# MLP2's finish: x added by accumulating transfers for the first two token blocks and half of the third, where VectorE added half, half and all

## The chip, the core and the metric

The kernel runs on one core of a Trainium2 chip. The metric is the device time of one execution in microseconds (us). TensorE (PE) multiplies, VectorE (DVE) and ScalarE (ACT) do the elementwise work, SyncE (SP) only issues transfers, and GpSimd (POOL) does nothing here but issue transfers of another kind: those that add what they bring to what lies in the destination.

## The reference

All tensors are float32; x has 2048 tokens of width 512.

```
xn = layernorm(x)
a  = xn @ dft_hid_re.T ; b = xn @ dft_hid_im.T
s  = dft_seq_re @ a - dft_seq_im @ b
h  = relu(xn @ w1 + b1) ** 2          # 512 -> 1792
g  = silu(h @ w2 + b2)                # 1792 -> 512
out = x + s * g
```

## The kernel before

Every operand is held as a high and a low part (`split`: ACT writes the high part, L69, DVE the low one, L72), and a product is three matmuls: high by high, high by low, low by high (`PASSES`). On top of that the large products are made blockwise, with seven products of sums of quarter blocks where eight would stand (`PRODUCTS`); the sums of operands (L201 to L209) and of results (`combine`, L240 to L243) are DVE's.

The order is written out by hand; each engine goes through its own list in order. First come the Fourier part (`products`, `mm`, `stage2`), which leaves s in four DRAM tiles `Y`, then MLP1 (`hidden`), which leaves the squared relu in DRAM tiles `HD`, and last MLP2, the loop over `units` from L785 on. It runs over four token blocks c of 512 tokens, and in each over seven slices p of 256 hidden features; n counts the 28 units. A unit is 42 matmuls (`outer`, L595) that need the unit's operand. `operand` makes it: SP loads it (`hr`, L566), DVE makes sums (L207 to L209), and ACT and DVE split it (L69, L72) into one of three places of the tile `block`. So at most three operands stand ready, and the seven results of a token block are summed up in PSUM over its seven units.

At the end of a token block, `combine` turns the seven sums into four quarters, k = 0 to 3, in the tile `z` (called `e` in the code, tag "e"): first ACT copies one sum into it (L239), then DVE does L240 to L243. The tile has a single buffer. The copy for the next block waits until all four quarters of the previous one are in DRAM. Behind this copy ACT writes the bias into the banks of the next block (L588); PE's second product of the block waits for one of those, for `m_b2` (shown as m_b_o) in blocks 1 and 2, and for the bank pair `m_12` (shown as m) in block 3.

A block's quarters are finished during the next block (`finish`): silu on ACT (L636), times s on DVE (L640), and then x is added in one of two ways. If x was loaded by `load_fin`, DVE adds it and SP issues the transfer to `out` (`plus`, L645 and L646). If not, POOL issues a transfer that adds x from DRAM into the quarter (L628), and SP issues the transfer to `out` later, at a place of its own (`put`, L631), once the adding transfer has landed. Before, k = 0 and 1 of blocks 0 and 1 and all of block 2 went the first way, and k = 2 and 3 of blocks 0 and 1 the second. The finish of block 2 thus lies in block 3, between the operands that PE needs there. Block 3 has a written-out tail (`rest`, `step`) with all four quarters on DVE.

Of the kernel before, what the change touches and what calls it, by code (L numbers as in the profile page):

```python
# [19 lines left out]
NTC = S // TC  # L20
# [42 lines left out]
def fnet_gated_kernel(ctx, tc, x, xt, ct, wd, w1, w2, b1, b2, out):  # L63
# [23 lines left out]
    def bank(tag, name):  # L87

        n = {"b3": 3, "b2": 2}.get(tag, 1)
        return acc.tile([P, n, 512], F32, tag=tag, name=name)  # L90

    def buf(tag, shape, name, dtype=F32, bufs=1):
        return pool.tile(shape, dtype, tag=tag, bufs=bufs, name=name)
# [383 lines left out]
    def load_w1(p):  # L477
        if p < NP - 1:
            t = sixth(2 + p, 2)
            nc.sync.dma_start(t.bitcast(F32), W1D[p])  # L480
            W1[p] = [t[:, :, n] for n in range(7)]
        else:
            a = buf("g0b", [P, 2, 3, 256], f"w1a_{p}", F32R)
            b = buf("g1b", [P, 2, 4, 256], f"w1b_{p}", F32R)
            nc.sync.dma_start(a.bitcast(F32), W1D[p][:, :, 0:3])
            nc.sync.dma_start(b.bitcast(F32), W1D[p][:, :, 3:7])
            W1[p] = [a[:, :, n] for n in range(3)] + [b[:, :, n] for n in range(4)]
# [96 lines left out]
    def bias(m, n, cols=slice(0, 2)):  # L584

        m = m.rearrange("p (k e) -> p k e", k=2)[:, cols]
        b = BIASED[n] * 256
        nc.scalar.activation(m, b2s[:, None, b:b + 256].to_broadcast([P, cols.stop - cols.start, 256]), AF.Copy)  # L588
# [13 lines left out]
    def at(src, k):  # L602

        h, b = WHERE[k]
        return src.rearrange("(h k p) (b e) -> h b p k e", h=2, k=2, b=2)[h, b]

    def load_fin(c):

        fin[c] = []
        for n, src in enumerate((Y[c], x[c * TC:(c + 1) * TC])):  # L610
            for m in range(2 if n == 0 or c > NTC - 3 else 1):
                tag = f"pq{n}{m}" if c < NTC - 1 else (("g0a", "sx"), ("g0b", "pq10"))[n][m]
                t = buf(tag, [P, 2, 512], f"fin{c}_{n}{m}")
                for i in range(2):
                    nc.sync.dma_start(t[:, i].rearrange("p (k e) -> p k e", k=2), at(src, 2 * m + i))
                fin[c].append(t)
# [13 lines left out]
    def put(c, e, k):  # L630
        nc.sync.dma_start(at(out[c * TC:(c + 1) * TC], k), e[:, k].rearrange("p (k e) -> p k e", e=256))  # L631
# [76 lines left out]
    def go(*names):  # L708


        for v in names:
            k, n = v[0], int(v[1:])
            if k == "m":
                load_rows(n, buf("pq00", [P, 4, 256], f"rows{n}"))
            elif k == "l":
                load_w2(n)
            elif k != "h" or n < len(units):
                if v not in making:
                    making[v] = {"h": lambda: operand(n, *units[n]), "x": lambda: tokens(n // 2, n % 2),
                                 "w": lambda: late_w2(n)}[k]()  # L720
                next(making[v])
# [28 lines left out]
    c = NTC - 1  # L750
# [8 lines left out]
    with ordered:  # L759
        before = None  # L760
        for n, (c, p) in enumerate(units):
            ahead, behind = beside.get((c, p), ((), ()))
            go(*ahead)
            unit = hidden(n, c, p)
            next(unit)
            if before:
                next(before)
            next(unit)
            go(*behind)
            before = unit  # L770
            if n == 0:
                stage2(NC - 1, 0)
                stage2(NC - 1, 1, "ba")
            if c == 0 and p + 4 < NP:
                load_w1(p + 4)
            if n == len(units) - 1:

                m26, m4 = bank("b2", "m_b2_o0"), bank("ba", "m_ba_o0")
                bias(m26[:, 0], 2)
                bias(m4[:, 0], 4)  # L780
        m753, m1 = bank("b3", "m_b3_o0"), bank("bb", "m_bb_o0")
        bias(m753[:, 1], 5)
        next(before)

        for n, (c, p) in enumerate(units):  # L785
            last = c == NTC - 1
            if n == 0:
                ms = m26, m753, m4[:, 0], m1[:, 0]
                at_ = product
            elif not last and p == 0:  # L790

                m4, m26, m753, m1 = (bank(tag, f"m_{tag}_o{c}") for tag in (("bb", "ba")[c - 1], "b2", "b3", "bc"))
                ms = m26, m753, m4[:, 0], m1[:, 0]
                bias(ms[2], 4)
                bias(product(ms, 2), 2)
                bias(product(ms, 5), 5)
            elif p == 0:

                m5, m40 = (bank(tag, f"m_{tag}_last")[:, 0] for tag in ("bb", "bc"))
                m12, m67 = bank("b2", "m_12"), bank("b3", "m_67")  # L800
                m3 = bank("ba", "m_ba_last")[:, 0]
                m4 = m40, m67[:, 2]
                ms = {1: m12[:, 0], 2: m12[:, 1], 6: m67[:, 0], 7: m67[:, 1], 5: m5, 3: m3}
                at_ = dict.__getitem__
                bias(m5, 5)
                bias(m40, 4, slice(0, 1))
                bias(ms[2], 2)
                bias(m4[1], 4, slice(1, 2))

            def add(k, p):  # L810
                if last and k == 4:
                    for i in range(2):
                        outer(m4[i], k, ready[c, p], p, (i,))
                else:
                    outer(at_(ms, k), k, ready[c, p], p)

            go(*{0: ("l4",), 1: ("w6",), 2: ("l5",)}.get(n, ()))
            if not last or p < REST:
                for k in ORDER if p else FIRST_LAST if last else FIRST:
                    add(k, p)  # L820
            if n == 1:

                nc.scalar.activation(stats[:, 0, 0, 0:1], stats[:, 0, 0, 0:1], AF.Silu)
            go(f"h{n + 3}")
            if p == NP - 1 and not last:
                e = buf("e", [P, 4, 512], f"z{c}")
                combine(e, ms)
                done_next = c, e
            if c and not last and p in (3, 4):
                put(*done, p - 1)  # L830
            go(f"h{n + 2}", *{2: ("w6",), 3: ("w6",)}.get(n, ()), f"h{n + 6}")
            if p == (3 if last else 5):
                load_fin(c)
            if p == NP - 1 and not last:
                done = done_next
            elif c:
                for k in ((2, 3), (0,), (1,), (), (), (), ())[p] if not last else ((), (0,), (1, 2), (3,), (), (), ())[p]:
                    finish(*done, k)


        e = buf("g1a", [P, 4, 512], f"z{c}")
        tail = NP - 1
        whole = slice(0, 512)
        w = [slice(i * 256, (i + 1) * 256) for i in range(2)]

        def rest(ks, ps=range(REST, NP)):
            for k in ks:
                for f in ps:
                    add(k, f)

        def step(to, a, b, op, w=whole):
            nc.vector.tensor_tensor(e[:, to, w], a[:, w], e[:, b, w], op=op)

        rest((1, 2, 6), range(REST, tail))
        rest((1, 2), (tail,))
        nc.scalar.activation(e[:, C21], ms[1], AF.Copy)
        step(C11, ms[2], C21, ALU.add)
        silu(e, C11)
        times(c, e, C11)
        plus(c, e, C11)  # L860
        rest((6,), (tail,))
        rest((7,))
        step(C22, ms[6], C21, ALU.add)
        step(C21, ms[7], C22, ALU.subtract)
        rest((5,))
        step(C12, m5, C22, ALU.subtract)
        step(C22, m5, C21, ALU.add)
        silu(e, C22)
        rest((3,))
        for f in range(REST, NP):  # L870
            outer(m4[0], 4, ready[c, f], f, (0,))
        times(c, e, C22)
        plus(c, e, C22)
        step(C12, m3, C12, ALU.add)
        silu(e, C12)
        step(C21, m4[0], C21, ALU.subtract, w[0])
        silu(e, C21, one)
        for f in range(REST, NP):
            outer(m4[1], 4, ready[c, f], f, (1,))
        times(c, e, C12)  # L880
        step(C21, m4[1], C21, ALU.subtract, w[1])
        silu(e, C21, two)
        times(c, e, C21, one)
        plus(c, e, C21, one)
        times(c, e, C21, two)
        plus(c, e, C21, two)
        plus(c, e, C12)
# [43 lines left out]
```

## Time and profile before

| | us |
|---|---|
| median of 3 runs (710.11, 710.51, 713.1) | 710.51 |
| the profiled execution's own time | 710.93 |
| its span, first to last instruction | 709.1 |
| PE busy, of the span | 687.0 |
| DVE busy | 584.5 |
| ACT busy | 347.3 |
| POOL, first accumulating transfer / last | 606.27 / 644.24 |
| MLP2's blocks 1, 2, 3 begin on PE at | 595.71, 630.57, 664.03 |

PE and DVE are so full that a difference can only come from a place where one waits for the other. A timeline row gives start, duration, engine, line, operation and tiles; in brackets stands how long the engine had been idle before it, and who ended that. In a windows row, after the stretch and its length, stand the busy time of PE, weight loads, DVE, ACT and POOL, then the TensorE clock that was granted (1.00 is full speed), and the DMA engines' share and rate.

### The profile page before, as it was taken

What the parts mean: (1) busy time and instruction counts of PE and PEld (TensorE: products, weight loads), DVE (VectorE), ACT (ScalarE), POOL (GpSimd) and SP (SyncE); (2) the same over time, 40 slices, a digit from 0 to 9 for tenths busy, and PEclk for the clock granted to TensorE, in tenths of its full rate; (3) what the DMA queues carried; (4) which work ended last, traced back from release to release, by engine and by line L of the source; (5) the groups of instructions that cost most, each with busy time, mean ns of one, the idle gap of its engine ahead of it and who ended that gap; (6) DMA issues with size and microseconds to landing.
All of it is one profiled execution on the core that took longest, in us unless ns stands there. A gap on an engine that the chain in (4) does not pass through costs nothing.

```text
span 709.1 us, 12790 instructions
## 1 busy us (share of the span) xinstructions
PE 687.0 (97%) x5179; PEld 647.7 (91%) x5179; DVE 584.5 (82%) x886; ACT 347.3 (49%) x475; POOL 5.2 (1%) x8
## 2 busy tenths in 40 slices
PE   8999999999999999999999998999999999999985
PEld 5778788999999999999999988899999998999985
DVE  7999654779598798797897737889999879999995
ACT  4437332444453544543543325667777754454431
POOL 0000000000000000000000000000000000101000
PEclk9999999999999999999999999999999999999998
DMA  9522441533653653835746809966724995667642
GB/s 333 216 90 90 155 131 42 216 108 138 214 204 134 254 177 134 310 112 194 262 122 233 328 11 366 351 223 208 269 119 164 350 417 193 187 218 208 239 149 88
DMA packets 55018, 141.09 MB, mean 199 GB/s; under 512 B 5040, under 2 KB 21680, under 8 KB 53680
## 3 DMA queue, kind: packets, MB, share of 16 engines
q1 hardware_dynamic: 49840, 124.56, 49.6%
q10 hardware_dynamic: 4032, 14.68, 5.1%
q0 software_dynamic: 1088, 1.05, 1.0%
q8 instruction: 40, 0.66, 0.4%
q14 instruction: 18, 0.15, 0.1%
HBM read 97.00 MB, written 43.27 MB: 198 GB/s over the span
## 4 chain that ended last, share of the span: by engine, by line
PE 73%; DVE 16%; DMA 6%; issue 2%; ACT 2%; SPq 0%; DVEq 0%; ACTq 0%
PE m_b L300 23%; PE yps L287 12%; PE hps L541 7%; PE m_b_o L595 7%; PE m_bb L300 5%; PE m_ba L300 5%; PE hps_b L541 4%; DVE block L72 4%; PE pq_b L353 3%; DMA w1b<-w1d 3%; PE hps_ba L541 2%; DVE g L72 2%; DMA w2raw<-in_w 2%; PE m_bc_o L595 1%; DMA xr<-in_xt 1%
## 5 line engine op out<-in xcount | busy, mean ns | idle before, releaser
L300 PE MATMUL m_b<-g,block 128*128 128x256 f32 x1080 | 129.0, 276 | 0.0
L300 PEld LDWEIGHTS m_b<-g,block 128*128 128x128 f32 x1080 | 125.5, 188 | 0.0
L69 ACT ACTIVATE g<-r 128x768 fp32r<-128x768 f32 (+2 forms) x65 | 57.4, 885 | 82.9 <-PE m_b L300 38.7
L72 DVE TENSOR_TENSOR g<-r,g 128x768 fp32r<-128x768 f32 (+2 forms) x65 | 65.5, 1007 | 36.0 <-ACT g L69 35.8
L287 PE MATMUL yps<-wd,pq 128*128 128x512 f32 (+1 forms) x414 | 92.9, 374 | 0.0
L287 PEld LDWEIGHTS yps<-wd,pq 128*128 128x128 f32 x414 | 74.8, 188 | 14.0
L72 DVE TENSOR_TENSOR g<-t,g 128x1024 fp32r<-128x1024 f32 x48 | 58.7, 1222 | 12.1 <-ACT g L69 12.1
L541 PE MATMUL hps<-xT,block 128*128 128x256 f32 x504 | 59.9, 278 | 0.0
L541 PEld LDWEIGHTS hps<-xT,block 128*128 128x128 f32 x504 | 58.7, 188 | 0.2
L69 ACT ACTIVATE g<-t 128x1024 fp32r<-128x1024 f32 x48 | 50.3, 1048 | 14.3 <-PE m_ba L300 6.5
L353 PE MATMUL pq_b<-g,block 128*128 128x512 f32 x180 | 47.6, 398 | 1.8 <-DVE g L72 1.7
L595 PE MATMUL m_b_o<-w,block 128*128 128x256 f32 x360 | 44.0, 278 | 2.3 <-ACT m_b_o L588 2.3
L552 ACT ACTIVATE h<-h,b1s 128x512 f32<-128x512 f32 x56 | 37.3, 715 | 18.1 <-DVE h L242 17.8
L300 PE MATMUL m_b<-g,xc 128*128 128x256 f32 x360 | 45.1, 277 | 0.0
L595 PEld LDWEIGHTS m_b_o<-w,block 128*128 128x128 f32 x360 | 42.2, 188 | 2.9 <-ACT m_b_o L588 2.9
L69 ACT ACTIVATE block<-hr 128x768 fp32r<-128x768 f32 (+1 forms) x28 | 35.5, 1268 | 18.4 <-DVE hr L209 9.3
L353 PEld LDWEIGHTS pq_b<-g,block 128*128 128x128 f32 x180 | 32.9, 188 | 11.3 <-DVE g L72 2.4
L300 PEld LDWEIGHTS m_b<-g,xc 128*128 128x128 f32 x360 | 42.9, 188 | 0.3
L72 DVE TENSOR_TENSOR block<-hr,block 128x768 fp32r<-128x768 f32 (+1 forms) x28 | 41.6, 1485 | 0.9 <-ACT block L69 0.8
L201 DVE TENSOR_TENSOR t<-r 128x512 f32<-128x512 f32 x48 | 32.9, 685 | 4.1 <-DMA r<-in_ct 3.9
L541 PE MATMUL hps_b<-xT,block 128*128 128x256 f32 x288 | 35.1, 278 | 0.0
L541 PEld LDWEIGHTS hps_b<-xT,block 128*128 128x128 f32 x288 | 34.1, 188 | 0.0
(200 smaller groups left out, 1182.6 us busy)
## 6 DMA issues: line engine op xcount, KB each, us to landing
r<-in_ct SPq DMA_DIRECT2D x63, 512.0 KB, 3.5
hd<-h ACTq DMA_DIRECT2D x28, 512.0 KB, 4.9
hr<-hd SPq DMA_DIRECT2D x28, 512.0 KB, 4.5
w1d<-w0g SPq DMA_DIRECT2D x21, 512.0 KB, 3.1
block<-w1d SPq DMA_DIRECT2D x6, 1792.0 KB, 8.8
block<-w2d SPq DMA_DIRECT2D x3, 1792.0 KB, 14.7
y<-ysb SPq DMA_DIRECT2D x16, 256.0 KB, 3.0
fin<-y SPq DMA_DIRECT2D x16, 256.0 KB, 4.5
```

What stands on the lines that cost most here:

```text
L69: nc.scalar.activation(hi, src, AF.Copy)
L72: return nc.vector.tensor_tensor(lo, src, hi.bitcast(F32), op=ALU.subtract)
L201: nc.vector.tensor_tensor(t[:, 0:2], r[:, 0:1].to_broadcast([P, 2, 256]), r[:, 1:3], op=ALU.add)
L287: nc.tensor.matmul(ps[:, s], PQ[c, m, k // 2][:, a_, w:w + P], WD[m, k][:, b_, s], start=n == 0, stop=n > len(todo) - 3, skip_group_check= ...
L300: nc.tensor.matmul(ps[:, d * CW:(d + 1) * CW], w[:, a_, d * P:(d + 1) * P], mv(b_), start=first and d == 0 and (a_, b_) == (HI, HI), stop= ...
L353: nc.tensor.matmul(accs[c][k], w, g[:, b_, 2 * h:2 * h + 2], start=j == 0 and h == 0 and (a_, b_) == (HI, HI), stop=j == NJ - 1 and h == 1 ...
L541: nc.tensor.matmul(product(ms, k), W1[p][a][:, a_, q * P:(q + 1) * P], xT[c, q][:, b_, b], start=share not in first, stop=q == 1 and (a_, ...
L552: nc.scalar.activation(x_[:, s], x_[:, s], AF.Relu, bias=b1s[:, f:f + 1])
L595: nc.tensor.matmul(m[:, k * 256:(k + 1) * 256], g[:, a_, a, k * P:(k + 1) * P], W2[p][:, b_, b], start=p == 0 and k == 0 and (a_, b_) == ( ...
```

## The change

Blocks 0 and 1 load no x for VectorE any more, and block 2 half of it; the finish of the third block begins with the two quarters that go by transfer; and the places of `put` are new.

```
-            for m in range(2 if n == 0 or c > NTC - 3 else 1):
+            for m in range(2 if n == 0 else (0, 0, 1, 2)[c]):
...
-            if c and not last and p in (3, 4):
-                put(*done, p - 1)
+            if c:
+                for k in ({4: (2,), 5: (3,)} if last else {3: (2, 3), 4: (0,), 5: (1,)}).get(p, ()):
+                    put(*done, k)
...
-                for k in ((2, 3), (0,), (1,), (), (), (), ())[p] if not last else ((), (0,), (1, 2), (3,), (), (), ())[p]:
+                for k in ((2, 3), (0, 1), (), (), (), (), ())[p] if not last else ((), (2,), (3, 0), (1,), (), (), ())[p]:
```

On POOL, whose list is nothing but these transfers (z0, z1, z2 are the tiles of blocks 0, 1, 2), the difference is this.

```order
-L628 DMA z0_6394<-in_x 128x2x256 x2
-L628 DMA z1_6785<-in_x 128x2x256 x2
-L902 UNCONDITIONAL_BRANCH
...
+L628 DMA z0_6391<-in_x 128x2x256 x4
+L628 DMA z1_6779<-in_x 128x2x256 x4
+L628 DMA z2_7171<-in_x 128x2x256 x2
+L903 UNCONDITIONAL_BRANCH
```

Four transfers of 256 KB became ten.

On SP, from the last operand load of block 1 (`hr1_6`) to the loads for the next finish, before (the number after hr is the block, the next one the slice):

```order
L566 DMA hr1_6_6460<-hd1_6_940 128x1024
L566 DMA hr2_0_6516<-hd2_0_941 128x1024
L646 DMA out_0<-z0_6394 128x2x256
L566 DMA hr2_1_6572<-hd2_1_942 128x1024
L646 DMA out_0<-z0_6394 128x2x256
L631 DMA out_0<-z0_6394 128x2x256
L566 DMA hr2_2_6628<-hd2_2_943 128x1024
L631 DMA out_0<-z0_6394 128x2x256
L566 DMA hr2_3_6678<-hd2_3_944 128x1024
L566 DMA hr2_4_6728<-hd2_4_945 128x1024
L615 DMA fin1_00_6730<-y1_67 128x2x256 x2
```

And with the change:

```order
L566 DMA hr1_6_6457<-hd1_6_940 128x1024
L566 DMA hr2_0_6513<-hd2_0_941 128x1024
L566 DMA hr2_1_6571<-hd2_1_942 128x1024
L631 DMA out_0<-z0_6391 128x2x256 x2
L566 DMA hr2_2_6624<-hd2_2_943 128x1024
L631 DMA out_0<-z0_6391 128x2x256
L566 DMA hr2_3_6674<-hd2_3_944 128x1024
L631 DMA out_0<-z0_6391 128x2x256
L566 DMA hr2_4_6725<-hd2_4_945 128x1024
L615 DMA fin1_00_6727<-y1_67 128x2x256 x2
```

The last transfer of z0 to `out` moved from ahead of `hr2_3` to behind it, and all four are now `put`s that wait for an accumulating transfer. The order for z1 in block 2 changes in the same way.

On DVE, in block 3, between the low parts of the operands of slices 4 (`hr3_4`) and 5 (`hr3_5`), before (fin2_00 and fin2_01 hold s, fin2_10 and fin2_11 hold x):

```order
L72 TENSOR_TENSOR block_78<-hr3_4_7120,block_78 128x1792
L640 TENSOR_TENSOR z2_7180<-z2_7180,fin2_00_7122 128x512
L645 TENSOR_TENSOR z2_7180<-z2_7180,fin2_10_7128 128x512
L640 TENSOR_TENSOR z2_7180<-z2_7180,fin2_01_7125 128x512
L645 TENSOR_TENSOR z2_7180<-z2_7180,fin2_11_7131 128x512
L207 TENSOR_TENSOR hs3_6_7401<-hr3_6_7249 128x512
...
L72 TENSOR_TENSOR block_78<-hr3_5_7188,block_78 128x1792
```

And with the change:

```order
L72 TENSOR_TENSOR block_78<-hr3_4_7114,block_78 128x1792
L640 TENSOR_TENSOR z2_7171<-z2_7171,fin2_01_7119 128x512
L640 TENSOR_TENSOR z2_7171<-z2_7171,fin2_00_7116 128x512
L645 TENSOR_TENSOR z2_7171<-z2_7171,fin2_10_7122 128x512
L207 TENSOR_TENSOR hs3_6_7390<-hr3_6_7240 128x512
...
L72 TENSOR_TENSOR block_78<-hr3_5_7179,block_78 128x1792
```

One addition (L645) is gone here, and one more ahead of `hr3_4`; the multiplications (L640) all stay.

## Prediction

> **What bounds the kernel now.** I read the busy shares first, then the windows by stage, then the timeline where PE has a hole. PE is the bound of the whole:
>
> ```profile
> PE 687.0 (97%) x5179; PEld 647.7 (91%) x5179; DVE 584.5 (82%) x886; ACT 347.3 (49%) x475; POOL 5.2 (1%) x8
> ```
>
> The change touches only MLP2 from its second token block on. These two windows are blocks 1 and 2, and block 3 with the tail:
>
> ```profile
> 594.60:663.40 68.80, 67.85 (x594) 67.38 (x594) 65.99 (x86) 33.29 (x38) 4.99 (x4) 1.00 0.68 200
> 663.40:709.10 45.70, 36.30 (x301) 35.71 (x300) 36.09 (x50) 14.66 (x20) 0.00 (x0) 0.92 0.47 160
> ```
>
> In blocks 1 and 2 PE lacks 0.95 us of 68.8, and that lies where block 1 begins, ahead of any line changed. DVE work taken out of these blocks buys nothing. Block 3's window lacks 9.4 us, most of it behind PE's last matmul, and its clock is 0.92. PE's timeline shows a hole within:
>
> ```profile
> 684.03 0.39 PE L595 MATMUL m<-w,block 128*128 128x256 f32 x2
> 686.76 0.74 PE L595 MATMUL m<-w,block 128*128 128x256 f32 x4 [2.34 <-DVE block L72]
> 687.33 0.84 PE L595 MATMUL m<-block 128*128 128x256 f32 x6
> 688.01 1.28 PE L595 MATMUL m<-w,block 128*128 128x256 f32 x6
> 689.09 1.48 PE L595 MATMUL m<-block 128*128 128x256 f32 x6
> 690.37 3.51 PE L595 MATMUL m<-w,block 128*128 128x256 f32 x24
> 693.72 0.84 PE L595 MATMUL m<-block 128*128 128x256 f32 x6
> ```
>
> PE arrives at 684.42 and waits 2.34 us for the low part of slice 5's operand. After that it is slow. The fine windows say why:
>
> ```profile
> 595.00:600.00 5.00, 4.05 (x33) 3.65 (x32) 4.76 (x6) 1.41 (x3) 0.00 (x0) 1.00 0.88 290
> ...
> 686.70:688.00 1.30, 1.24 (x10) 1.24 (x11) 1.26 (x4) 0.00 (x0) 0.00 (x0) 1.00 1.00 316
> 688.00:690.00 2.00, 2.00 (x13) 2.00 (x12) 2.00 (x3) 0.00 (x0) 0.00 (x0) 0.56 0.88 269
> 690.00:692.00 2.00, 2.00 (x12) 2.00 (x12) 0.04 (x1) 0.00 (x0) 0.00 (x0) 0.59 1.04 347
> 692.00:694.00 2.00, 2.00 (x20) 2.00 (x19) 0.07 (x1) 0.60 (x1) 0.00 (x0) 1.00 0.42 148
> ```
>
> The granted clock falls to about half from 688.0 for some 3.4 us, just behind the hole. The hole of 0.95 us in the first row cost no clock. The chain of waits gives the normal pace, and what carries the end after the hole:
>
> ```profile
> 655.35 3.40 PE m_b_o L595 x30
> ...
> 693.30 0.61 ACT z L856
> ```
>
> At 3.40/30 = 0.113 us each, the 46 matmuls from 686.76 to 693.72 need 5.21 us; they took 6.96. The slow clock cost 1.75 us. From 693.30 the chain runs through ACT and DVE, which start when PE's first products are done, so all that PE wins by then reaches the end.
>
> **What the change removes.** These DVE rows are the path to that hole:
>
> ```profile
> 663.55 1.22 DVE L241 TENSOR_TENSOR z<-m_b_o,z 128x1024 f32<-128x1024 f32 x1 [0.68 <-PE m_b_o L595]
> ...
> 676.45 0.69 DVE L645 TENSOR_TENSOR z<-z,fin 128x512 f32<-128x512 f32 x1
> 677.06 0.68 DVE L207 TENSOR_TENSOR hr<-hr 128x512 f32<-128x512 f32 x1
> ...
> 684.69 2.02 DVE L72 TENSOR_TENSOR block<-hr,block 128x1792 fp32r<-128x1792 f32 x1
> ...
> 689.09 0.95 DVE L72 TENSOR_TENSOR block<-hr,block 128x768 fp32r<-128x768 f32 x1
> ```
>
> DVE is without a gap from 663.55 to 686.71, where PE resumes. Of six additions removed, only the two of block 2 lie on it. One costs 677.06 - 676.45 = 0.61 us, so the operand comes **1.22 us** earlier and the hole shrinks from 2.34 to 1.12 us, near the 0.95 that kept the clock: **1.75 us** more. What is late next is slice 6's operand, ready at 690.04, or 688.82 with the change; PE, resuming at 685.54, wants it 30 matmuls (3.40 us) later, at 688.94. It just holds. The other four additions (2.4 us of DVE) cover nothing: the next thing DVE waits for is PE. Taken alone, the change would give 2.97 us.
>
> **What it adds.** Six accumulating transfers, and with them a longer way until z is free. POOL's rows, DVE's around them, and the landing times of accumulating transfers (L628) and of `put` (L631), shortest, median and longest:
>
> ```profile
> 606.27 1.33 POOL L628 DMA_DIRECT2D z<-in_x  x1 [605.82 <-DVE z L640]
> 611.17 1.22 POOL L628 DMA_DIRECT2D z<-in_x  x1 [3.57 <-DVE z L640]
> 639.86 1.21 POOL L628 DMA_DIRECT2D z<-in_x  x1 [27.47 <-DVE z L640]
> 644.24 1.23 POOL L628 DMA_DIRECT2D z<-in_x  x1 [3.17 <-DVE z L640]
> ```
>
> ```profile
> 605.27 1.29 DVE L640 TENSOR_TENSOR z<-z,fin 128x512 f32<-128x512 f32 x2
> ...
> 630.09 1.23 DVE L241 TENSOR_TENSOR z<-m_b_o,z 128x1024 f32<-128x1024 f32 x1 [0.76 <-PE m_b_o L595]
> ...
> 638.81 1.29 DVE L640 TENSOR_TENSOR z<-z,fin 128x512 f32<-128x512 f32 x2
> 640.02 0.68 DVE L207 TENSOR_TENSOR hr<-hr 128x512 f32<-128x512 f32 x1
> ```
>
> ```profile
> DMA to landing us min/median/max: 4.1/5.1/6.0
> ```
>
> ```profile
> DMA to landing us min/median/max: 2.8/4.3/5.5
> ```
>
> Both multiplications of a pair are done at 606.56 and 640.10, yet the second transfer starts only at 611.17 and 644.24. The releaser that the rows name had been done for 4 us; what fits is the first transfer's landing. I take it that POOL starts one accumulating transfer when the last has landed: every 4.90 or 4.38 us, 4.64 in the mean. With four in a row, block 0's last starts at 611.17 + 2 x 4.64 = 620.45, lands 5.1 later at 625.55, and the last `put`, waiting for it on SP, lands at 625.55 + 4.3 = **629.85**. Queued behind this `put` on SP are slice 4's operand, which DVE takes up at 640.02, and the loads for the next finish, wanted from 638.81; they have room. ACT's copy into z (L239) has none:
>
> ```profile
> 626.69 0.60 ACT L239 ACTIVATE z<-m_bc_o 128x512 f32<-128x512 f32 x1 [3.56 <-PE m_bc_o L595]
> ...
> 629.38 0.60 ACT L588 ACTIVATE m_b_o<-b2s 128x512 f32<-128x512 f32 x1
> ...
> 660.15 0.60 ACT L239 ACTIVATE z<-m_bc_o 128x512 f32<-128x512 f32 x1 [3.55 <-PE m_bc_o L595]
> ...
> 663.06 0.59 ACT L588 ACTIVATE m<-b2s 128x512 f32<-128x512 f32 x1
> ```
>
> ```profile
> 631.25 1.52 PE L595 MATMUL m_b_o<-w,block 128*128 128x256 f32 x12
> ...
> 664.03 1.52 PE L595 MATMUL m<-w,block 128*128 128x256 f32 x12
> ```
>
> Before, the last `put` was issued at 619.32, so the copy waited for PE alone:
>
> ```profile
> 619.32 0.39 SPq L631 DMA_DIRECT2D out<-z  x1
> ```
>
> Behind the copy ACT stands in one row up to the bias that PE's second product needs: done at 629.98, which is 3.29 after the copy's start. PE wants it at 631.25, so the copy may start at 627.96. It starts at 629.85: **PE loses 1.9 us**. On DVE, L240 follows the copy's 0.60 and takes 1.23 like L241, which then starts at 631.7: DVE is 1.6 late against 630.09. In block 2 the same, from 639.86 + 1.6 = 641.5: the fourth transfer goes out at 655.4 and lands at 660.5, the `put` at 664.8. Bias there ends 3.50 after the copy, PE wants it at 664.03 + 0.68 = 664.71, plus the 1.9; the copy may start at 663.1. **Another 1.7** for PE, 3.6 in all. DVE's L241 starts at 664.8 + 0.60 + 1.23 = 666.6, 3.1 later than 663.55.
>
> **The sum** for block 3: the operand of slice 5 is ready at 686.71 + 3.1 - 1.22 = 688.6; PE arrives at 684.42 + 3.6 = 688.0, waits 0.6, and resumes 1.9 us later than before, with its clock kept: 1.9 - 1.75 = +0.15. The profiled execution's own 710.93 becomes 711.1. It lay 0.42 above the median, so I forecast **710.7**: gain and loss cancel.
>
> Bounds: with the shortest rows (4.38, 4.1, 2.8) the first `put` lands at 626.8 and nothing is late, which is rival 1; with the longest (4.90, 6.0, 5.5) it lands at 632.5, PE loses 4.5 there, DVE is 8.5 late in block 3, and the end is 8.5 - 1.2 - 1.75 = 5.6 later, 716.1. I take means and medians, since eight transfers and eight `put`s in a row average out; 708.5 to 713 is the forecast's own range.
>
> **Rivals.** 1: z is free in time. If POOL's second start was set by something else, four transfers go out 1.2 us apart, the last `put` lands before 623, and all 2.97 us are won: 707.96, less 0.42, **707.5**. Against it stand both late starts; for it, that two spacings are few, and that they were taken among loads the change moves.
>
> The Trainium skill ("Perfetto Trace Analysis", section "DMA Instruction — SWDGE (GPSIMD)") has the profiled end of such an instruction at the last descriptor written; by that POOL was through at 607.60 and could go on, which is rival 1. The row 611.17 speaks against it.
>
> 2, the slower one: the clock falls at the seams too. PE's new stalls of 1.9 and 1.7 us where blocks 2 and 3 begin lie between the 0.95 us that cost no clock and the 2.34 that did; from a point in between, each costs 1.75 us: 712.4 with one, **714.2** with both.
>
> The Trainium skill ("TensorE: Matmul & The Clock Gate", "What's actually happening") has the clock halved after an idle window of about 3.4 us that runs free of the program; by that alone neither stall would cost clock. The trace disagrees: 2.34 us of idling did.
>
> 3: z is in time, but the 1.12 us that remain still drop the clock: only 1.22 us won, 709.7, less 0.42, **709.3**. That the change doesn't do what it says is excluded by the lists: the additions are gone.
>
> **How the numbers follow.** Forecast 0.50, rival 1 0.22, rival 2 0.18, rival 3 0.10. The range 707.2 to 714.6 takes in all four centres and leaves out the long tail above. Half a per cent, about what a measurement of this kernel can tell, is 3.55 us. Faster by more (below 706.96) needs rival 1 and the rest of the hole besides: 0.06. Slower by more (above 714.06) is rival 2 with both drops and the forecast's tail: 0.18. The rest, 0.76, is no difference.
>
> **What would show it.** POOL's rows: a spacing of 4 to 5 us in a run of four, or 1.2. ACT's copy L239 of blocks 2 and 3: released by a transfer to `out`, near 630 and 665, or by PE as now. PE where its second product begins: a wait for ACT's bias of 1 to 3 us, or none. The wait for the operand of slice 5: 0.6 us, and the clock at 1.00 behind it. The forecast is wrong if POOL doesn't take its transfers one by one, or if landings among the moved loads are much shorter or longer than these medians.

## The result, and the profile after

The changed kernel takes 720.6 us (median of 6 runs, 718.23 to 721.96) where the kernel before takes 710.42 beside it (6 runs, 710.06 to 713.1): 1.0136 times as long, with an interval of 1.0116 to 1.0156, about 10 us. The forecast was 710.7, and the range ended at 714.6. The profiled execution took 720.11 us, its span is 718.3 against 709.1. Of all runs behind this document the intervals leave one out, which took 853.7 us at a granted clock of 0.75: it is among the 12 of the first kernel with more room.

The line of busy times on the page, then two windows that answer to those of blocks 1 and 2 and of block 3 with the tail (stretch, its length, busy time of PE, PEld, DVE, ACT, POOL, the granted clock, DMA share, GB/s):

```profile
PE 689.6 (96%) x5179; PEld 649.9 (90%) x5179; DVE 580.4 (81%) x880; ACT 346.9 (48%) x475; POOL 12.5 (2%) x14
```

```profile
594.10:671.95 77.85, 71.13 (x597) 70.23 (x595) 62.19 (x81) 30.04 (x33) 9.88 (x8) 0.96 0.65 170
671.95:718.30 46.35, 35.29 (x296) 34.91 (x294) 36.02 (x49) 17.90 (x24) 2.44 (x2) 0.91 0.55 169
```

DVE has 4.1 us less to do, as the lists say. Yet blocks 1 and 2 take 77.85 us instead of 68.8; PE lacks 6.72 of them, where it lacked 0.95. Block 3 with its tail takes 46.35, for 45.70. PE's timeline has the place of the loss. First rows of the kernel before that weren't shown, then their counterparts after:

```profile
629.89 0.84 PE L595 MATMUL m_bb_o<-w,block 128*128 128x256 f32 x6
...
635.47 0.84 PE L595 MATMUL m_bc_o<-w,block 128*128 128x256 f32 x6
...
663.35 0.84 PE L595 MATMUL m_ba_o<-w,block 128*128 128x256 f32 x6
...
669.07 2.88 PE L595 MATMUL m<-w,block 128*128 128x256 f32 x24
...
701.20 0.84 PE L595 MATMUL m<-w,block 128*128 128x256 f32 x6
```

```profile
629.39 0.84 PE L595 MATMUL m_bb_o<-w,block 128*128 128x256 f32 x6
634.61 1.65 PE L595 MATMUL m_bc_o<-w,block 128*128 128x256 f32 x6 [4.38 <-ACT z L239]
637.30 2.93 PE L595 MATMUL m_b_o<-w,block 128*128 128x256 f32 x12 [1.04 <-ACT m_b_o L588]
640.02 1.48 PE L595 MATMUL m_ba_o<-w,block 128*128 128x256 f32 x6
...
643.41 0.84 PE L595 MATMUL m_bc_o<-w,block 128*128 128x256 f32 x6
...
671.29 0.84 PE L595 MATMUL m_ba_o<-w,block 128*128 128x256 f32 x6
675.76 2.93 PE L595 MATMUL m<-w,block 128*128 128x256 f32 x12 [3.63 <-ACT m L588]
...
682.14 2.88 PE L595 MATMUL m<-w,block 128*128 128x256 f32 x24
...
697.10 0.84 PE L595 MATMUL m<-w,block 128*128 128x256 f32 x6
...
710.02 0.84 PE L595 MATMUL m<-w,block 128*128 128x256 f32 x6
```

A seam is the place where one block ends on PE and the next begins. Row against row, PE is 0.50 us ahead at the end of block 1 (its last six matmuls at 629.39 for 629.89), 7.94 behind after the first seam, at the second unit of block 2 (643.41 for 635.47), no more than that at the end of block 2 (671.29 for 663.35), 13.07 after the second seam, at the second unit of block 3 (682.14 for 669.07), and 8.82 at its last row (710.02 for 701.20). So the first seam costs 8.44, the second 5.13, and block 3 gives 4.25 back: at 697.10 PE starts on slice 5's operand without a wait, where it had waited 2.34. The half clock is at the seams now:

```profile
634.60:640.60 6.00, 4.95 (x21) 4.66 (x22) 5.76 (x6) 4.75 (x7) 0.00 (x0) 0.50 0.78 283
675.80:678.40 2.60, 2.60 (x12) 2.60 (x13) 2.50 (x3) 1.65 (x3) 0.00 (x0) 0.50 0.89 314
697.00:699.00 2.00, 2.00 (x20) 2.00 (x19) 2.00 (x3) 0.68 (x1) 0.00 (x0) 1.00 1.13 340
```

Why ACT's copy is late is read from POOL's rows, SP's `put` (L631) and the copy itself:

```profile
605.77 1.34 POOL L628 DMA_DIRECT2D z<-in_x  x1 [605.33 <-DVE z L640]
610.89 1.23 POOL L628 DMA_DIRECT2D z<-in_x  x1 [3.77 <-DVE z L640]
619.21 1.21 POOL L628 DMA_DIRECT2D z<-in_x  x1 [7.09 <-DVE hr L208]
625.63 1.23 POOL L628 DMA_DIRECT2D z<-in_x  x1 [5.22 <-DVE hs L207]
...
655.36 1.21 POOL L628 DMA_DIRECT2D z<-in_x  x1 [3.82 <-DVE hs L208]
663.92 1.22 POOL L628 DMA_DIRECT2D z<-in_x  x1 [7.35 <-issue]
```

```profile
611.77 7.58 SPq L631 DMA_DIRECT2D out<-z  x2
619.44 0.42 SPq L566 DMA_DIRECT2D hr<-hd  x1
625.33 0.37 SPq L631 DMA_DIRECT2D out<-z  x1
...
631.27 0.37 SPq L631 DMA_DIRECT2D out<-z  x1
```

```profile
633.96 0.60 ACT L239 ACTIVATE z<-m_bc_o 128x512 f32<-128x512 f32 x1 [11.57 <-DMA out<-z]
...
672.21 0.60 ACT L239 ACTIVATE z<-m_bc_o 128x512 f32<-128x512 f32 x1 [7.92 <-PE m_ba_o L595]
```

The starts lie 5.12, 8.32 and 6.42 us apart in block 0 and 4.58, 5.04 and 8.56 in block 1. The trace has the landings at 610.62, 618.94, 625.31, 631.25 and 650.01, 655.04, 663.61, 669.66: each start but the first of a block comes 0.26 to 0.32 us behind the landing ahead of it. Block 0's last `put` lands at 633.86, block 1's at 672.11; the copies start 0.10 later. In the second row the releaser is not the one that counts: the sum that the copy reads, m_bc_o, was done at 668.05. The chain of waits names it rightly, and shows what sets the end from there:

```profile
663.92 5.74 DMA z<-in_x
...
669.67 2.43 DMA out<-z
...
672.21 0.60 ACT z L239
...
672.84 1.23 DVE z L240
```

### The profile page after: what moved, and what is told of

Same layout as the page of the kernel before. It is cut to its first block, busy times and chain, and to the rows that moved or that the text cites. A ratio compares the mean times of both kernels' runs of the same rounds, so it can differ in the third digit from the quotient of the medians.

```text
span 718.3 us, 12788 instructions
## 1 busy us (share of the span) xinstructions
PE 689.6 (96%) x5179; PEld 649.9 (90%) x5179; DVE 580.4 (81%) x880; ACT 346.9 (48%) x475; POOL 12.5 (2%) x14
```

## The experiments

Four questions: are the seams all of the loss; why does POOL take its transfers one by one; why did they land so much later than the rows before said; and what of a seam's price is stall, what clock. Each median below stands beside runs of the kernel before on the same chip, whose medians were 710.36 for the first three kernels and the first one with more room, 710.89 for the next two with room, the puts and the first matmuls, 710.98 for the room alone, the loads and 52 matmuls, and 710.85 for the last.

**Only block 2's half by transfer, only block 0 by four, and a z of its own for block 1**

```diff
-            for m in range(2 if n == 0 else (0, 0, 1, 2)[c]):
+            for m in range(2 if n == 0 else (1, 1, 1, 2)[c]):
```

The finish of blocks 0 and 1 is as in the kernel before.

> Only block 2's part of the change: blocks 0 and 1 finish as before (two additions by VectorE, two by transfer). Theory A (the loss of 10 us lies where blocks 2 and 3 begin, because ACT's copy L239 waits until the last put of the old z has landed): no put is later than before, the copies at about 626.7 and 660.2 wait for PE as before, and what is left is the gain in block 3. Against the trace before, PE in the changed kernel makes up 13.07 - 8.82 = 4.25 us between slice 5's first matmuls and 703.2, and loses 0.38 behind them: 710.5 - 3.9 = 706.6, between 705.5 and 708. Theory B (the accumulating transfers as such cost the time, by the traffic that they add and displace, wherever they stand): block 2 has a third of the six that were added, so a third of the loss stays, 710.5 + (13.6 / 3) - 4 = about 711.

```diff
-            for m in range(2 if n == 0 else (0, 0, 1, 2)[c]):
+            for m in range(2 if n == 0 else (0, 1, 2, 2)[c]):
```

The finish of blocks 1 and 2 is as in the kernel before.

> Only block 0's part: its x is added by four transfers, blocks 1 and 2 finish as before. Theory A: the whole price of the first seam and nothing else: PE's row after it stood 635.47 before and 643.41 in the changed kernel, which was 0.50 ahead there, so 8.4 us; the second seam is as before and the hole in block 3 stays. 710.5 + 8.4 = 719 (717 to 720). PE waits for ACT's copy L239 by 3 to 5 us near 630, with the granted clock at 0.50 behind it. Theory B (traffic as such): a third of the loss of 13.6 us, 715, and not in one place.

```diff
-                e = buf("e", [P, 4, 512], f"z{c}")
-                combine(e, ms)
+                if c == 1:
+                    e = Apart(buf("pq11", [P, 2, 512], "z1a"), buf("pq10", [P, 2, 512], "z1b"))
+                    combine_apart(e, ms)
+                else:
+                    e = buf("e", [P, 4, 512], f"z{c}")
+                    combine(e, ms)
```

`Apart` sends quarters 0 and 1 to the first tile, 2 and 3 to the second.

> The change whole, but block 1's z gets a place of its own (two tiles that the change left free), so that no block's copy has to wait for the puts of the block just ahead; the six transfers more stay, one by one as now. The first steps of DVE's combination go by 512 columns instead of 1024, in seven instructions instead of four. Theory A: both seams are as before (copies released by PE), the gain of block 3 stays: 706.6, between 705.5 and 708.5; POOL's spacing stays at 4.5 to 8.5 us. Theory B (the transfers cost the time by their traffic): 720 as in the changed kernel, or a few us less.

Measured: **708.59** (12 runs), 0.9977 of before (0.9964 to 0.9991); **719.66** (5 runs), 1.0135 (1.0112 to 1.0158); **708.45** (12 runs), 0.9973 (0.9962 to 0.9985). PE's waits in the timelines of the three, in this order, and the clock behind the last:

```profile
686.02 0.74 PE L595 MATMUL m<-w,block 128*128 128x256 f32 x4 [0.89 <-DVE block L72]
```

```profile
636.02 1.07 PE L595 MATMUL m_bc_o<-w,block 128*128 128x256 f32 x6 [3.38 <-ACT z L239]
638.71 2.93 PE L595 MATMUL m_b_o<-w,block 128*128 128x256 f32 x12 [1.62 <-ACT m_b_o L588]
...
697.63 0.78 PE L595 MATMUL m<-w,block 128*128 128x256 f32 x4 [2.35 <-DVE block L72]
```

```profile
684.89 0.74 PE L613 MATMUL m<-w,block 128*128 128x256 f32 x4 [0.91 <-DVE block L72]
```

```profile
686.00:688.00 2.00, 2.00 (x20) 2.00 (x20) 2.00 (x3) 0.00 (x0) 0.00 (x0) 1.00 1.09 347
```

The third kernel has all six transfers more, one by one as before (POOL's starts in block 1: 639.50, 644.32, 649.51, 658.13), and is faster than the kernel before. So it isn't traffic: the loss is the hand-over of z, theory A. Block 0 alone costs 9.3 us, what the first seam was to cost and a little more. The gain is smaller than expected, 1.9 us and not 3.9: I had read 4.25 from a kernel in which PE comes late enough to find slice 5's operand ready. Without seams a hole of 0.9 us stays, and the clock behind it is 1.00.

**More room for POOL's descriptors**

```diff
-    b2s = pool.tile([P, D], F32, name="b2s")
...
+            if n == len(units) - 2:
+                b2s = held["b2s"] = buf("pq11", [P, D], "b2s")
+                nc.sync.dma_start(b2s, bcast(b2, D))
...
-    nc = bacc.Bacc("TRN2", target_bir_lowering=False, num_devices=1, dynamic_dma_scratch_size=1024)
+    nc = bacc.Bacc("TRN2", target_bir_lowering=False, num_devices=1, dynamic_dma_scratch_size=3072)
```

> The change whole, but POOL's room for descriptors in SBUF is 3072 bytes of a partition instead of 1024; to make that room the bias row of W2 is kept in a tile that is free by then and loaded late in MLP1. One transfer has 272 packets on 16 rings, 17 each. If POOL starts its next transfer only when the last has landed because the descriptors of two don't fit, then with three times the room the starts follow each other by the 1.22 to 1.33 us of the instruction: four are issued by 611 and 651, the last put is out before 622 and 660, both seams vanish, 706.6. If POOL waits for the landing whatever the room, the spacing stays 4.5 to 8.5 us and the time 720.

Measured: 711.27 (12 runs), 1.0004 (0.999 to 1.0018). POOL's starts fall together in pairs (608.65 and 609.49, 613.30 and 614.03), and PE has no wait at a seam; but the bias row, loaded late, holds PE up where MLP2 begins, a flaw of the edit; its row in the timeline:

```profile
563.94 2.93 PE L594 MATMUL m_b_o<-w,block 128*128 128x256 f32 x12 [5.05 <-ACT m_b_o L587]
```

So the same with the load five units earlier (`n == len(units) - NP + 1`), the same with all of block 2 by transfer, and the room alone without the change.

> The change whole with 3072 bytes of room for POOL's descriptors, as in the run before, but the bias row is loaded five units earlier in MLP1. There its late load held PE for 5.05 us at 563.9, and everything behind was 2.4 us later than in the kernel before. Theory A (room for descriptors makes POOL serial, the serial transfers make z late, late z makes both seams): no wait of PE at the seams, the hole ahead of slice 5 shrinks to 0.9 us with the clock at 1.00 behind it, and without the 2.4 us the time is that of the kernel with a place of its own for block 1's z, 708.4 (707 to 709.5). If the larger room costs something else, it stays at 711.

```diff
-            for m in range(2 if n == 0 else (0, 0, 1, 2)[c]):
+            for m in range(2 if n == 0 else (0, 0, 0, 2)[c]):
...
-                for k in ({4: (2,), 5: (3,)} if last else {3: (2, 3), 4: (0,), 5: (1,)}).get(p, ()):
+                for k in ({4: (2,), 5: (3,), 6: (0, 1)} if last else {3: (2, 3), 4: (0,), 5: (1,)}).get(p, ()):
```

> As the run beside it (3072 bytes of room, bias row loaded early), and block 2's x is added by four transfers too, no addition by VectorE left but block 3's. Theory A: two additions of 0.61 us fewer on DVE's path to slice 5's operand, so the 0.9 us that are left of the hole go: 0.9 less than the run beside it, about 707.5. Rival: the 0.9 us are not DVE's additions but DMA or ACT (the loads of block 3's y and x, which the transfers now meet), and the time is the same or up to 2 us longer.

> The kernel before, with nothing of the change, but with the 3072 bytes of room for POOL's descriptors and the bias row loaded early in MLP1. Its second transfers then start 0.7 us behind the first ones instead of 4.4 to 4.9, and z is free earlier, but nothing waited for it. Theory A: no difference, 710.5 (709.7 to 711.3), the hole of 2.3 us ahead of slice 5 and the slow clock behind it are there. Rival: the room itself is worth something, and part of the gain of the two runs with room and change is its own: 709.

Measured: **709.09** (12 runs), 0.9979 (0.9963 to 0.9995); **707.71** (12 runs), 0.9964 (0.995 to 0.9978); **710.99** (12 runs), 0.9996 (0.9977 to 1.0015). POOL's block 0 in the first of them (two transfers in a row), then PE's wait ahead of slice 5 in each:

```profile
605.33 2.57 POOL L627 DMA_DIRECT2D z<-in_x  x2 [604.89 <-DVE z L639]
609.98 2.44 POOL L627 DMA_DIRECT2D z<-in_x  x2 [2.08 <-DVE z L639]
```

```profile
685.56 0.74 PE L594 MATMUL m<-w,block 128*128 128x256 f32 x4 [0.89 <-DVE block L72]
```

```profile
685.51 0.74 PE L594 MATMUL m<-w,block 128*128 128x256 f32 x4 [0.17 <-DVE block L72]
```

```profile
687.36 0.73 PE L594 MATMUL m<-w,block 128*128 128x256 f32 x4 [2.37 <-DVE block L72]
```

With three times the room a second start follows 0.72 to 0.85 us behind the first, long before that has landed, and a pair starts 0.3 to 0.4 us behind DVE's multiplication (ended at 609.68, start at 609.98). Only the room and the place of the bias row differ, and the starts are no longer serial: the room is their cause, and the reading is that two transfers' descriptors don't fit the 1024 bytes. The room alone is worth nothing, and with it the change becomes a gain. All of block 2 by transfer takes the rest of the hole (0.17 of 0.89) and is the best version, 3.2 us below the kernel before.

In the kernel with the room alone half of what was expected didn't come: the hole ahead of slice 5 is there, 2.37 us long, but the clock behind it stays at full speed, where it had fallen to 0.56 in the kernel before.

```profile
688.00:690.00 2.00, 2.00 (x20) 2.00 (x20) 2.00 (x3) 0.00 (x0) 0.00 (x0) 1.00 0.96 285
```

The Trainium skill ("Perfetto Trace Analysis", "DMA Instruction — SWDGE (GPSIMD)") ends such an instruction at its last descriptor, not at the landing. The traces agree with either room: POOL's rows of one transfer last 1.2 to 1.7 us, and the landing comes 4 us and more after the start. So the wait for room shows in none of POOL's rows; with 1024 bytes only the distance of the starts tells of it.

**Puts held together, and loads put beside a transfer**

```diff
-                for k in ({4: (2,), 5: (3,)} if last else {3: (2, 3), 4: (0,), 5: (1,)}).get(p, ()):
+                for k in ({4: (2,), 5: (3,)} if last else {5: (2, 3, 0, 1)}).get(p, ()):
```

> The change whole, but the four puts of block 0 and of block 1 go out together behind the fourth accumulating transfer. It asks why the third and fourth transfer of a run took 6.1, 5.6, 8.2 and 5.7 us to land where the first took 4.3 to 4.9. Theory D (the transfers of SP that go out when the one before lands, the put and behind it a load of 512 KB, are served first): without the puts among them these four land in 4 to 5.5 us, the fourth of block 0 by about 629, that of block 1 by about 664, and z is free at about the same time or 2 us earlier, 718 to 721. Theory E (a transfer is slower by its place in the row): they stay at 5.6 to 8.2 us, and z is free later by three more puts, 722 to 726.

Measured: 718.02 (4 runs), 1.0111 (1.0088 to 1.0134). The edit didn't do what it was meant to: SP sent the puts whose quarters had landed just as the fourth transfer started. The transfers took 4.68, 7.13, **4.28**, 7.19 us in block 0 and 4.68, 4.26, **4.91**, 8.46 in block 1. The third, now without a put beside it, is among the fast ones; the fourth, with three, is slow. Place in the row (theory E) is out; half of the expectation, four fast landings, was wrong. Still z is free 1.67 us earlier in block 0 (its last `put` lands at 632.19 for 633.86).

The last one puts a measured dose beside a transfer that had none. It is the kernel with only block 2's half by transfer, with three loads that nothing reads:

```diff
+        if c == NTC - 2 and k == 2:
+            more = buf("pq11", [P, 2, 512], "more")
+            for t in (fin[c][1][:, 0], more[:, 0], more[:, 1]):
+                nc.sync.dma_start(t.rearrange("p (k e) -> p k e", k=2), at(x[c * TC:(c + 1) * TC], k))
         nc.gpsimd.dma_start(z, at(x[c * TC:(c + 1) * TC], k), accum_op=ALU.add)
```

> The kernel with only block 2's half by transfer, where the first accumulating transfer of block 2 landed after 4.25 us with no other traffic beside it (five such transfers in the runs so far took 4.17 to 4.36). Here SP issues three loads of 256 KB, which nothing reads, at the moment at which POOL issues that transfer. Theory D (SP's transfers issued at that moment are served first): it lands after 5.6 to 6.1 us, as the third and fourth transfers of a run did, which had 787 KB beside them. Theory E (place in the row, or POOL's writing of descriptors): 4.2 to 4.4 us as before. The time is not the question, within 1 us of 708.6.

SP's loads and POOL's transfer here, and the landing time of this one transfer, without the loads and with them:

```profile
675.76 0.38 SPq L631 DMA_DIRECT2D fin<-in_x  x1
676.19 0.98 SPq L631 DMA_DIRECT2D more<-in_x  x2
```

```profile
676.15 1.21 POOL L632 DMA_DIRECT2D z<-in_x  x1 [31.21 <-DVE z L644]
```

```profile
DMA to landing us min/median/max: 4.2/4.2/4.2
```

```profile
DMA to landing us min/median/max: 6.5/6.5/6.5
```

4.25 became 6.52 us: what SP sends beside a transfer makes it late, a little more than theory D expected. That all of it is served first isn't shown: the first packet moved 2.46 us after the start, for 1.92 without the loads, and the third load landed just ahead of the transfer. (One run, 707.12 us, and one transfer.) Over the 56 transfers of seven kernels with 1024 bytes (before, after, and those of the first, the puts' and the first matmuls' experiment), the straight line through the landing times is 3.6 us plus 2.9 for each MB that other queues moved until a microsecond before the landing, with a correlation of 0.88. It is a rough fit: transfers with nothing beside them took 4.2 to 4.4 us.

**Matmuls in the seams**

```diff
+                if c == 2:
+                    fill(ms[2], c, 38)
                 bias(ms[2], 4)
...
+                fill(m5, c, 32)
                 bias(m5, 5)
```

`fill` issues so many matmuls on operands at hand.

> The change whole, but PE runs 38 matmuls at the first seam and 32 at the second whose results are written over by the bias that follows, 0.113 us each, so that it doesn't idle while the copy L239 waits. It splits the price of a seam into stall and clock. Theory A (idling lets the clock fall): the clock stays at 1.00 at both seams, the copies and the waits for ACT's bias stay where they are, and PE gets back what the slow matmuls cost behind the last wait: (2.93 - 1.52) + (1.48 - 0.84) = 2.05 us at the first seam and (2.93 - 1.52) + (1.09 - 0.84) = 1.66 at the second, 3.7 in all, 716.9. Theory C (the clock falls there for another cause than idling): 720.6 as the changed kernel, with the clock at 0.50.

Measured: 720.18 (4 runs), 1.0142 (1.0119 to 1.0166). A miss by 3.3 us. At the first seam the clock stayed at 1.00, and PE was 1.88 us earlier behind it (its row stands at 641.53, for 643.41). Block 1's transfers started at the same times as before (645.77 for 645.74), and the second seam took the 1.88 back. There 32 matmuls weren't enough:

```profile
637.33 1.65 PE L595 MATMUL m_b_o<-w,block 128*128 128x256 f32 x12 [1.71 <-ACT m_b_o L588]
...
675.81 2.25 PE L595 MATMUL m<-w,block 128*128 128x256 f32 x12 [1.93 <-ACT m L588]
```

```profile
677.00:680.00 3.00, 3.00 (x16) 3.00 (x16) 3.00 (x3) 1.84 (x3) 0.00 (x0) 0.50 0.54 189
```

With 52 in the second seam:

> As the run with matmuls in the seams, but 52 in the second seam instead of 32, since with 32 PE still idled 1.93 us there and the clock fell to 0.50 behind it. Theory A (the slow clock at the second seam reaches the end): the clock stays at 1.00 at both seams, PE is 1.7 us earlier behind the second one, and the time is 718.5. Theory F (the second seam's place is set by the transfers and DVE alone, as it was when the first seam's 1.88 us came back there): PE is earlier behind the second seam but meets DVE's operand of slice 5 again, a wait of about 1 to 2 us appears there, and the time stays at 720.

Measured: 719.97 (4 runs), 1.0112 (1.0081 to 1.0143). The clock stayed at 1.00, but it tells nothing between the theories: the bias of the matmuls' own bank waited for them, and ACT's later biases with it, so that PE's products began at 677.61. Then with 50, and that bias third:

```diff
-                bias(m5, 5)
-                bias(m40, 4, slice(0, 1))
+                fill(m5, c, 50)
                 bias(ms[2], 2)
+                bias(m40, 4, slice(0, 1))
+                bias(m5, 5)
```

> As the run with 52 matmuls in the second seam, which held back the bias of their own bank and with it all biases of ACT behind it, so that PE's products began at 677.6 instead of 675.8: here 50, and that bias is the third instead of the first, the one that the first products need is the first. Theory A (the slow clock at the second seam reaches the end): clock 1.00, products from 675.8 on at full pace, 1.7 us gained behind the seam, 718.4. Theory F (DVE is next): the low part of slice 5's operand was ready at 696.2 and PE came at 697.1, so only 0.9 us of the 1.7 can reach the end; PE waits 0.8 us there, and the time is 719.2 to 720.

Measured: 719.78 (4 runs), 1.0123 (1.0107 to 1.014). Products from 676.05 at full pace, and then, as theory F had it, a wait for DVE at slice 5:

```profile
694.59 2.02 DVE L72 TENSOR_TENSOR block<-hr,block 128x1792 fp32r<-128x1792 f32 x1
```

```profile
696.66 0.74 PE L595 MATMUL m<-w,block 128*128 128x256 f32 x4 [0.50 <-DVE block L72]
```

At both seams the slow clock is real and is worth about 1 us of the 10 (the row behind this wait stands at 697.24 for 697.78, and the medians are 0.8 apart, or 1.3 if each is set against the kernel before beside it): with it away, DVE, as late as z made it, sets the end.

## Why the prediction was wrong, step by step

- **What bounds the kernel: right for the hole, open for the clock.** A hole of 2.3 to 2.4 us ahead of slice 5 is in the kernel before and with the room alone, and it shrinks in every kernel that takes DVE's additions away without a seam. But the slow clock doesn't follow from the hole's length: with the room alone the hole of 2.37 us left it at 1.00. So the 1.75 us are what the one trace of before shows, and not what every such hole costs; what decides was not found.
- **The gain of 2.97 us: right in the trace.** With a z of its own for block 1, PE's last row stands at 697.71 for 701.20; 0.56 of that it had ahead where block 1 begins (596.64 for 597.20), which leaves 2.9. The hole was to be 1.12 and is 0.91, with the clock kept. Repeated runs give less, 1.1 to 2.7 us; the one profiled execution of before lay 0.4 above its median and that of this kernel 0.7 below. That the clock doesn't always fall in the kernel before either would explain it too, but only one execution of it was profiled.
- **POOL takes its transfers one by one: right**, to 0.3 us behind each landing, with a cause that the prediction left open, the room for descriptors.
- **"With four in a row, block 0's last starts at 611.17 + 2 x 4.64 = 620.45, lands 5.1 later at 625.55, and the last `put` [...] lands at 625.55 + 4.3 = 629.85": this is the step that failed.** The mechanism is right, the spacing is mis-sized. The last transfer started at 625.63 and the `put` landed at 633.86, in a kernel that was 0.5 us ahead: 4.5 late. The three spacings, 5.12, 8.32 and 6.42 us for 4.90 and twice 4.64, make 5.7 of it and the last landing, 5.62 for 5.1, makes 0.5; the `put` itself took 2.59 for 4.3 and hid 1.7. In block 1 the `put` landed at 672.11 for 664.8. The 4.64 came from the first transfer of each pair, which has few transfers beside it. A later one starts at the very landing that lets a `put` of 256 KB out, and behind that `put` SP sends a load of 512 KB (619.21 beside 618.96 and 619.44, 625.63 beside 625.33 and 625.80); two loads went out ahead of block 0's second transfer, and two puts and two loads around block 1's third. The second transfers in the trace of before had landed after 5.98 and 5.47 us. In the prediction's upper bound, 632.5 and 716.1, the 6.0 stands for the last landing alone, with a spacing of 4.90 still; 633.86 in a kernel 0.5 ahead lies beyond that bound. And the bound was dismissed because eight transfers average out. They don't: what makes a later one late comes back with each.
- **A copy later than 627.96 costs PE one for one: right.** Less 0.50, that is 627.46; the copy started at 633.96, 6.50 late. PE lost 8.44, of which 1.88 was clock by the run with matmuls: 6.56. At the second seam the copy could start 3.50 ahead of 664.71, later by PE's 7.94: 669.15. It started 3.06 after that, and with the 1.66 of slow matmuls that is 4.72 of the 5.13.
- **The sum: the order of its two terms didn't hold.** PE was to come to slice 5's operand 0.6 us before it was ready. The operand was ready at 694.17 + 2.02 = 696.19, 9.48 later than before, and PE came to it at 697.10, 0.91 after that. So PE's own lateness set the end: 13.07 us after the second seam, less 4.25, is 8.82 at its last row, and the span is 9.2 longer.
- **Rival 1, z in time, 707.5:** not this kernel, but what the change comes near to once POOL has room (709.1) or z has (708.5).
- **Rival 2, the clock falls at the seams too:** it did, at both. Its price was wrong: 3.5 us were added for it, and it is worth about 1, since DVE was next.
- **Rival 3, what remains of the hole still drops the clock:** it didn't; behind the 0.89 and 0.91 us that remain the clock is 1.00.

What stays open: which of the transfers beside one of POOL's holds it up most, and whether a smaller room than 3072 bytes would do; neither was tried.

## What to carry to other kernels

Before more work goes to a queue that the profile shows nearly idle, read how far apart its starts lie: if a start follows each landing, look for what the queue has run out of, here room for descriptors. Mending that (709.1) and mending the hand-over behind it (708.5) each took the loss away. Size a transfer in a row by those rows of the trace that had the same neighbours, not by the mean of all; when the same event releases the transfer and its neighbours, the longest row is the estimate and no bound. And when a late hand-over feeds a second engine, taking the first engine's stall away only shows the second one.

## What the runs showed of the hardware

- With 1024 bytes of descriptor room POOL started a transfer of 256 KB (272 packets) 0.26 to 0.32 us behind the landing of the last (once 0.44, where DVE's multiplication ended just after that landing); with 3072, three were under way, started 0.72 to 0.85 us apart within a pair. The third and fourth of block 0 landed 9.8 and 12.2 us after their starts, with SP's traffic beside them, and still in time.
- A transfer of POOL's with none beside it landed after 4.15 to 4.36 us; its first packet moved 1.9 us after the start. With 1.2 to 1.5 MB of SP's beside it, it took up to 8.5, and up to 4.6 went by before the first packet. The Trainium skill ("DMA: Bandwidth & Descriptors", "SWDGE vs HWDGE vs iDMA") has each DMA engine go round its queues in turn; by that alone the first packet would not be late. The traces agree only once it has moved: after the start at 610.89, none of its packets moved from 612.12, where POOL's row ends, to 614.85, while SP's did, and from then on both queues moved in each microsecond. From 612.50 to 614.50 the DMA engines were busy for only 0.36 of the time, so engines taken by SP don't explain that wait; its cause is open.
- How long PE idled did not alone decide about its clock. It fell behind 1.93 us (second seam, 32 matmuls), 2.34 (before) and 2.35 (only block 0 by four); it stayed at 1.00 behind 1.71 (first seam, 38 matmuls) and behind 2.37 (the room alone), one time each.
